# Random-feature attention and a feed-forward block on one core: new start times for the queries, two of four normalisations on ScalarE, and output products two slices behind

## The chip, the core and the metric

The kernel runs on one core of one Trainium2 chip. A core has TensorE (PE: matmuls, with its weight loads as PEld), VectorE (DVE), ScalarE (ACT), GpSimd (POOL) and SyncE (SP), which issues nearly all DMAs here. Each engine works through its own queue in a fixed order, and semaphores hold an instruction until what it reads is there. The metric is the device time of one execution in microseconds (us), lower is better.

## The reference, cut to what matters

```
phi(x): h = x @ omega.T - sum(x*x)/2;  exp(h - max(h)) / sqrt(m)
kv  = einsum('bhsm,bhsd->bhmd', phi(k), v);   z = sum over s of phi(k)
out = einsum('bhsm,bhmd->bhsd', phi(q), kv) / (einsum('bhsm,bhm->bhs', phi(q), z) + 1e-6)
x   = out, heads joined: 4608 x 512
h   = x @ w_in;   g = h - tanh(h);   result = g @ w_out        (w_in 512 x 2048, w_out 2048 x 512)
```

There are 8 batches of 576 tokens and 8 heads of 64; m is 128.

## The kernel before

**Number format.** A float32 value is kept as two parts, a rounded high part and the low rest (`xh`, `xl`; `gh`, `gl`), and a product is three matmuls: high by high, high by low, low by high.

**Attention units.** The work of attention is cut in Python generators that other code advances a step at a time. `k_unit(b, c)` makes, for batch b and head pair c, the matrix `kvw` and the sums `zb`. `q_unit(ch, c)` takes 256 tokens (chunk ch) of a head pair: it loads, splits the input in halves (L132, L133 for the low parts), projects (`pj`), makes the exponentials (L149 on DVE, L153 on ACT), multiplies with `zb` and adds up (L350), takes the reciprocal (L353), scales four 128x128 blocks by it (L359 on DVE, L357 on ACT; the list `norm` says which), transposes on PE (`pt`, L366), splits again (`qh`, `ql`, L385), multiplies with `kvw` (`pn`, L391 and L392) and writes the result to `later` (ACT L396, L397, then DVE L398, L399). `pt` and `pn` share PSUM places, so the next unit's transposes wait until L399 has read this unit's `pn`. `x_split` (L407 on ACT, L408 on DVE) turns a head pair of `later` into `xh` and `xl`, which the feed-forward part reads. `xh` and `xl` hold two chunks: a chunk's number modulo 2 is its place.

**Feed-forward.** Chunks 0 and 1 go together, then chunks 2 to 5 one by one, eight slices each (`ffn_h(ch, s)`: 24 matmuls of 128x256 into a PSUM tile h, L471, then tanh on ACT L475, the subtraction on DVE L476, the two parts by L477 and L478; `ffn_out`: 12 matmuls of 128x512, L489 to L491). Then six pairs of chunks of 512 tokens, the wide part, 16 slices each (`wide_h(a, f)`: 12 matmuls of 128x512, L532, tanh L535, subtraction L536, parts L537, L538, and on POOL L540, L541; `wide_out`: 6 matmuls, L545 to L547; after the 16 slices the other half of the tokens, `last`). The h tiles have two PSUM banks in turn, so a slice's matmuls wait for the subtraction two slices earlier.

**What sets the order.** A counter `t` goes up at each `beat()`, two beats a slice; chunk 2 begins at 32, each chunk takes 16, the wide part begins at 96 and a pair takes 40. `start` holds, for each value of t, the units that begin there. A unit takes a step at every tick after that. `next_x(a)` forces ticks until the eight query units of a pair have ended, and splits them. From these calls a scheduler makes the order of each engine when the program is built; the order is fixed in the program.

Of the kernel before, what the change touches and what calls it, by code (L numbers as in the profile page):

```python
# [19 lines left out]
P = 128  # L20
# [5 lines left out]
C0 = 6  # L26
# [8 lines left out]
def favor_attention_ffn(ctx: ExitStack, tc: tile.TileContext, qT, kT, va, vt, omT, w, out):  # L35
# [283 lines left out]
    def q_unit(ch, c):  # L319
# [68 lines left out]
        for h in range(2):  # L388
            for b, s, e in pieces:
                w = kvs[b, c][0][:, h * P : (h + 1) * P]  # L390
                nc.tensor.matmul(pn[:, h, s:e], w, qh[:, h, s:e], start=True, stop=False)  # L391
                nc.tensor.matmul(pn[:, h, s:e], w, ql[:, h, s:e], start=False, stop=True)  # L392
        while ch >= C0 and gathered < (ch - C0) // 2:
            yield
        xs = later[:, c, ch % 2 * TC : ch % 2 * TC + TC]
        nc.scalar.copy(xs[0:D], pn[D:P, 0])  # L396
        nc.scalar.copy(xs[D:P], pn[0:D, 1])  # L397
        nc.vector.tensor_add(xs[0:D], pn[0:D, 0], xs[0:D])  # L398
        nc.vector.tensor_add(xs[D:P], pn[D:P, 1], xs[D:P])  # L399
        if ch < C0:  # L400
            yield
            x_split(ch, c, xs, nc.vector)
        xdone[ch] = xdone.get(ch, 0) + 1

    def x_split(ch, c, x, engine):
# [121 lines left out]
    def wide_h(a, f):  # L527
        p = ps.tile([P, 2, TC], F32, tag=bank("h"), name=f"h_w{a}_{f}")
        prods = [(w_in(a, f, i, c), x[:, 0:2, c]) for c in range(NC)
                 for i, x in ((0, xh), (0, xl), (1, xh))]  # L530
        for i, (w_, x) in enumerate(prods):
            nc.tensor.matmul(p, w_, x, start=i == 0, stop=i == len(prods) - 1)  # L532
        g = sb.tile([P, 2, TC], F32, tag=bank("o"), name=f"g_w{a}_{f}", bufs=1 if mode["o"][-1] == "g" else 2)
        e = sb.tile([P, 2, TC], F32R, tag="gh", name=f"ge_w{a}_{f}", bufs=2)
        nc.scalar.activation(g, p, AF.Tanh)  # L535
        nc.vector.tensor_sub(g, p, g)  # L536
        nc.scalar.copy(e[:, 0], g[:, 0])  # L537
        nc.vector.tensor_sub(e[:, 1], g[:, 0], e[:, 0].bitcast(F32))  # L538
# [17 lines left out]

    need = {b: (b * S) // TC for b in range(B)}
    xdone = {}
    gathered = 0
    gens = []  # L560

    def tick(new=(), force=False):
# [39 lines left out]
    while decoded < NF:  # L602
# [24 lines left out]
    kvf.clear()  # L627
    ak = open_pool("ak")
    mode.update(
        chain=False, native=False, norm=[nc.vector, nc.vector, nc.vector, nc.scalar], junk=[junk],  # L630
        hi=nc.scalar, pj=["pj0"], pk=["pk"], pt=["pj0"],
        phi=(ak, 3), qh=(ak, 1), ql=(ak, 1), kf=(ak, 1), kx=(ak, 1), qf=(ak, 1),
        qx=(ak, 1), vr=(ak, 1), khl=(ak, 2), vhl=(ak, 2), zs=(ak, 1), c1=(ak, 1), kvs=(ak, 1))
# [5 lines left out]
    def begins(a):  # L639

        return 16 * C0 + 40 * a

    for ch in range(3, NQ):
        a, j = (ch - C0) // 2, (ch - C0) % 2 * NC
        for c in range(NC):
            if ch < C0 + 2:
                k = [(28,32,36,40),(41,45,49,53),(56,60,63,66),(58,68,72,75),(78,81,83,85)][ch - 3][c]
            else:
                k = begins(a - 1) + -9 + 10 * (j + c) // 2
            start.setdefault(k, []).append(("q", ch, c))  # L650
    for b in range(2, B):
        a = ((b * S) // TC - C0) // 2
        for c in range(NC):
            k = [31,51][b - 2] + [5,5][b - 2] * c if b < 2 + len([31,51]) else begins(a - 1) + -18 + 11 * c
            start.setdefault(k, []).append(("k", b, c))
    t = 32 - 2 * (NF - done)
    assert min(start) >= t and all(k == int(k) for k in start)
# [11 lines left out]
    ffn_store(0)  # L669
    mode.update(pj=["pj0", "pj1"], pt=["pt"])  # L670
    prev = None
    for ch in range(2, C0):
        out_tiles(ch)
        for s in range(NS):
            while ch > 2 and xdone.get(ch, 0) < NC:
                tick((), True)
            g = (ch, s, *ffn_h(ch, s))
            beat()
            if prev is not None:
                ffn_out(*prev)  # L680
# [84 lines left out]
```

## Time and profile before

| | us |
|---|---|
| median of three runs | 1074.54 |
| lowest and highest | 1073.91, 1076.31 |
| the profiled execution's own time | 1075.36 |
| its span, first to last instruction | 1073.6 |
| PE busy | 1041.5 |
| DVE busy | 854.3 |
| ACT busy | 695.0 |
| POOL busy | 440.9 |

The profile comes from one execution. Its span and its time differ by 1.8 us. Busy time is the union of an engine's instructions; a matmul's row lasts until its result is written, so two matmuls in a row overlap, and a busy PE has not shown that it lost nothing.

### The profile page before, as it was taken

How to read it: one execution, taken by the hardware profiler on the slowest of the kernel's cores; microseconds unless marked ns; L12 is line 12 of the kernel's file. 1: busy time of each engine (PE TensorE's matmuls, PEld its weight loads, DVE VectorE, ACT ScalarE, POOL GpSimd, SP SyncE). 2: the span in 40 equal slices, each digit the busy share in tenths (PEclk: the TensorE clock that was granted, in tenths of full speed). 3: DMA queues.
4: the chain of work that ended last, by engine and by line, in shares of the span. 5: the costliest groups of instructions: out<-in, count | busy, mean ns of one | idle time of the engine just before them, and what ended most of it. 6: DMA issues, size and time to landing. Idle time of an engine off the chain costs nothing.

```text
span 1073.6 us, 19114 instructions
## 1 busy us (share of the span) xinstructions
PE 1041.5 (97%) x5608; PEld 889.1 (83%) x5608; DVE 854.3 (80%) x3006; ACT 695.0 (65%) x1809; POOL 440.9 (41%) x745
## 2 busy tenths in 40 slices
PE   8988999999999899899999999999999999999998
PEld 7766888999988898688888888888887888888886
DVE  5999995999999989989989888899889958742220
ACT  5997655777777778677767676677666746532220
POOL 3634540544543322556545563656355402221320
PEclk8999999999999999899999999999999999999999
DMA  8952722111211101222234332443243314332301
GB/s 261 295 172 90 283 96 70 33 34 53 55 53 33 53 16 57 72 77 78 78 109 137 103 118 88 130 138 117 65 142 115 104 45 146 114 101 82 104 1 39
DMA packets 85960, 106.18 MB, mean 99 GB/s; under 512 B 17632, under 2 KB 67936, under 8 KB 83808
## 3 DMA queue, kind: packets, MB, share of 16 engines
q1 hardware_dynamic: 85776, 104.92, 31.1%
q8 instruction: 45, 0.74, 0.3%
q14 instruction: 59, 0.48, 0.1%
q10 hardware_dynamic: 80, 0.03, 0.0%
HBM read 87.10 MB, written 17.83 MB: 98 GB/s over the span
## 4 chain that ended last, share of the span: by engine, by line
PE 67%; DVE 22%; issue 5%; ACT 4%; POOL 1%; DMA 0%; DVEq 0%; POOLq 0%; ACTq 0%
PE h_w L532 19%; PE h L471 7%; PE last L545 4%; PE last L547 4%; PE last L546 4%; DVE junk L350 3%; PE po_w L547 3%; PE po_w L546 3%; PE po_w L545 3%; PE po L489 2%; PE po L490 2%; PE po L491 2%; PE pk L269 2%; PE pt L366 2%; DVE phi_q L359 2%
## 5 line engine op out<-in xcount | busy, mean ns | idle before, releaser
L532 PE MATMUL h_w<-xh,w 128*128 128x512 f32 x768 | 253.9, 394 | 2.7 <-DVE g_w L536 2.6
L532 PEld LDWEIGHTS h_w<-xh,w 128*128 128x128 f32 x768 | 144.1, 189 | 31.1 <-DVE g_w L536 4.2
L532 PE MATMUL h_w<-xl,w 128*128 128x512 f32 x384 | 151.3, 394 | 0.9 <-DVE xl L408 0.9
L471 PE MATMUL h<-xh,w 128*128 128x256 f32 (+1 forms) x640 | 147.2, 307 | 3.8 <-DVE g L476 2.2
L540 POOL CAST w<-g_w 128x256 fp32r<-128x256 f32 x96 | 41.0, 427 | 224.2 <-DVE g_w L536 208.5
L471 PEld LDWEIGHTS h<-xh,w 128*128 128x128 f32 x640 | 107.5, 190 | 11.8 <-DVE g L476 3.1
L350 DVE CUSTOM_DVE_ANT_0 junk<-phi_q,zb 128x128 f32<-128x128 f32 (+1 forms) x320 | 105.3, 331 | 13.1 <-ACT phi_q L153 1.0
L536 DVE TENSOR_TENSOR g_w<-h_w,g_w 128x512 f32<-128x512 f32 x96 | 66.0, 687 | 60.6 <-ACT g_w L535 59.9
L471 PE MATMUL h<-xl,w 128*128 128x256 f32 (+1 forms) x320 | 97.5, 305 | 2.1 <-DVE xl L408 2.1
L153 ACT ACTIVATE phi_q<-phi_q,nb_q 128x128 f32<-128x128 f32 x240 | 82.5, 394 | 19.6 <-DVE nb_q L149 18.7
L535 ACT ACTIVATE g_w<-h_w 128x512 f32<-128x512 f32 x96 | 56.8, 591 | 57.1 <-PE h_w L532 53.4
L253 POOL TENSOR_TENSOR khl<-phi_ka,khl 128x256 fp32r<-128x256 f32 x48 | 38.3, 798 | 127.3 <-DVE khl L252 105.5
L532 PEld LDWEIGHTS h_w<-xl,w 128*128 128x128 f32 x384 | 72.8, 190 | 14.4 <-DVE xl L408 1.3
L541 POOL TENSOR_TENSOR w<-g_w,w 128x256 fp32r<-128x256 f32 x96 | 80.0, 833 | 4.6
L440 POOL TENSOR_SCALAR a<-a 128x1024 f32<-128x1024 f32 x14 | 59.0, 4213 | 54.4 <-ACT a L436 36.0
L545 PE MATMUL po_w<-w,ge_w 128*128 128x512 f32 x192 | 75.9, 395 | 0.0
L545 PE MATMUL last<-w 128*128 128x512 f32 x192 | 75.4, 393 | 0.0
L546 PE MATMUL po_w<-w,ge_w 128*128 128x512 f32 x192 | 75.3, 392 | 0.0
L547 PE MATMUL last<-w 128*128 128x512 f32 x192 | 75.2, 392 | 0.0
L546 PE MATMUL last<-w 128*128 128x512 f32 x192 | 75.1, 391 | 0.0
L537 ACT CAST ge_w<-g_w 128x256 fp32r<-128x256 f32 x96 | 39.1, 407 | 55.6 <-DVE g_w L536 53.9
L547 PE MATMUL po_w<-w,ge_w 128*128 128x512 f32 x192 | 72.2, 395 | 1.3 <-DVE ge_w L538 1.2
(173 smaller groups left out, 2911.9 us busy)
## 6 DMA issues: line engine op xcount, KB each, us to landing
w<-w_in SPq DMA_DIRECT2D x320, 128.0 KB, 2.4
raw<-w SPq DMA_DIRECT2D x16, 1024.0 KB, 8.1
kf<-kT SPq DMA_DIRECT2D x32, 288.0 KB, 3.2
qf<-qT SPq DMA_DIRECT2D x72, 128.0 KB, 2.2
out<-o SPq DMA_DIRECT2D x36, 256.0 KB, 2.1
w_in<-w SPq DMA_DIRECT2D x16, 512.0 KB, 3.4
v<-vt SPq DMA_DIRECT2D x24, 288.0 KB, 2.9
v<-va SPq DMA_DIRECT2D x8, 288.0 KB, 5.9
```

The costliest lines, as they stand in the source:

```text
L153: nc.scalar.activation(ph[:, j], ph[:, j], AF.Exp, bias=nb[:, j : j + 1], scale=-1.0)
L350: nc.vector.tensor_tensor_reduce(bank("junk")[r], ph[r, i], kvs[b, c][1][r, h], scale=1.0, scalar=EPS, op0=ALU.mult, op1=ALU.add, accum_ou ...
L440: engine.tensor_scalar(a.bitcast(F32), a.bitcast(F32), 2.0**-15, 122879.9921875, op0=ALU.max, op1=ALU.min)
L471: nc.tensor.matmul(o, w_, x, start=i == 0, stop=i == len(prods) - 1)
L532: nc.tensor.matmul(p, w_, x, start=i == 0, stop=i == len(prods) - 1)
L535: nc.scalar.activation(g, p, AF.Tanh)
L536: nc.vector.tensor_sub(g, p, g)
L540: nc.gpsimd.tensor_copy(hi, g[:, 1])
L541: nc.gpsimd.tensor_sub(lo, g[:, 1], hi.bitcast(F32))
L545: nc.tensor.matmul(o, h, wt[f][:, 0, DM:], start=f == 0, stop=False)
L546: nc.tensor.matmul(o, h, wt[f][:, 1, DM:], start=False, stop=False)
L547: nc.tensor.matmul(o, l, wt[f][:, 0, DM:], start=False, stop=f == NF - 1)
```

## The change

It has five parts. The first two are in the tables of starts: query units of chunks 3 to 9 and key units of batches 2 to 4 begin at other beats. For chunks 3 to 7 (row by row, four head pairs each) and for the key units:

```diff
-k = [(28,32,36,40),(41,45,49,53),(56,60,63,66),(58,68,72,75),(78,81,83,85)][ch - 3][c]
+k = [(28,31,34,37),(43,46,49,52),(40,55,58,63),(61,66,69,72),(75,78,80,83)][ch - 3][c]
...
-                k = begins(a - 1) + -9 + 10 * (j + c) // 2
+                k = begins(a - 1) + (-4 + 9 * (j + c) // 2 if a == 1 else -9 + 5 * (j + c))
...
-            k = [31,51][b - 2] + [5,5][b - 2] * c if b < 2 + len([31,51]) else begins(a - 1) + -18 + 11 * c
+            k = [28,48,82][b - 2] + [5,5,9][b - 2] * c if b < 2 + len([28,48,82]) else begins(a - 1) + -18 + 11 * c
```

The split of a chunk leaves the query unit and is made by the main loop, a slice after the chunk is there; a query unit now writes `later` as soon as the chunk two earlier has been split:

```diff
-        while ch >= C0 and gathered < (ch - C0) // 2:
+        while ch > 3 and ch - 2 not in split:
             yield
...
-        if ch < C0:
-            yield
-            x_split(ch, c, xs, nc.vector)
...
+    def x_of(ch):
+        split.add(ch)
+        for c in range(NC):
+            x_split(ch, c, later[:, c, ch % 2 * TC : ch % 2 * TC + TC], nc.vector)
...
+            if s > 0 and ch + 1 not in split and xdone.get(ch + 1) == NC:
+                x_of(ch + 1)
             g = (ch, s, *ffn_h(ch, s))
+            if ch == C0 - 1 and s == NS - 1 and xdone.get(C0 + 1) == NC:
+                x_of(C0 + 1)
```

Two of a query unit's four normalisations go to ScalarE where one did; the wide part's output products come a slice later, with three places for `e` where there were two and two for `g` where there were three:

```diff
-        chain=False, native=False, norm=[nc.vector, nc.vector, nc.vector, nc.scalar], junk=[junk],
+        chain=False, native=False, norm=[nc.vector, nc.scalar], junk=[junk],
...
-        g = sb.tile([P, 2, TC], F32, tag=bank("o"), name=f"g_w{a}_{f}", bufs=1 if mode["o"][-1] == "g" else 2)
-        e = sb.tile([P, 2, TC], F32R, tag="gh", name=f"ge_w{a}_{f}", bufs=2)
+        g = sb.tile([P, 2, TC], F32, tag="gl", name=f"g_w{a}_{f}", bufs=2)
+        tag = ("gh", "gh", "g")[f % 3]
+        e = sb.tile([P, 2, TC], F32R, tag=tag, name=f"ge_w{a}_{f}", bufs=len(tag))
...
         for f in range(NF):
-            g = wide_h(a, f)
+            behind.append(wide_h(a, f))
             beat()
-            if prev is not None:
-                wide_out(*prev)
+            if f > 1:
+                wide_out(*behind.pop(0))
```

What the scheduler makes of it shows at two places. The first is DVE ahead of the first slice of chunk 4. `later<-pn_4_3` is the last query unit of that chunk, and the `xl_101` behind it its split, for which that slice's last matmuls wait. Before:

```order
L398 TENSOR_TENSOR later_102<-pn_4_3_3512,later_102 64x256
L399 TENSOR_TENSOR later_102<-pn_4_3_3512,later_102 64x256
L252 CAST khl_3_1_0_3525<-phi_ka3_1_3470 128x2x128
L408 TENSOR_TENSOR xl_101<-later_102,xh_100 128x256
L252 CAST khl_3_1_2_3531<-phi_ka3_1_3470 128x2x128
L311 TENSOR_TENSOR kvs_3_0_3581<-pk_3_0_3121,kvs_3_0_3581 128x128
```

and in the changed program, where L405 is what was L408:

```order
L398 TENSOR_TENSOR later_102<-pn_4_3_3583,later_102 64x256
L399 TENSOR_TENSOR later_102<-pn_4_3_3583,later_102 64x256
...
L262 TENSOR_TENSOR vhl_3_1_4_3597<-v_3_1_3257,vhl_3_1_4_3597 64x64
L132 TENSOR_TENSOR qx_5_2_3644<-qf_5_2_3606,qx_5_2_3644 64x256
L262 TENSOR_TENSOR vhl_3_1_4_3597<-v_3_1_3257,vhl_3_1_4_3597 64x64
L133 TENSOR_TENSOR qx_5_2_3644<-qf_5_2_3606,qx_5_2_3644 64x256
...
L262 TENSOR_TENSOR vhl_3_1_5_3700<-v_3_1_3257,vhl_3_1_5_3700 128x2x64
L405 TENSOR_TENSOR xl_101<-later_102,xh_100 128x256
```

One instruction stood between the unit's end and its split; now there are thirteen, of other units, four of them exponent preparations (L149, left out above with their short read-outs).

The second place is PE in the second wide pair. `h_w1_4` is slice 4, `ge_w1_2` what slice 2 hands to its output products. Before:

```order
L532 MATMUL h_w1_4_7421<-xh_100,w8_1133 128x512
L532 MATMUL h_w1_4_7421<-xl_101,w8_1133 128x512
L545 MATMUL po0_w_7140<-w2_448,ge_w1_2_7304 128x512
L305 MATMUL pk_5_1_6948<-ident_64,c1_5_1_7191 128x128 x2
L307 MATMUL pk_5_1_6948<-zhl_5_1_7188,ones_92 128x256 x2
L546 MATMUL po0_w_7140<-w2_448,ge_w1_2_7304 128x512
L547 MATMUL po0_w_7140<-w2_448,ge_w1_2_7304 128x512
```

and in the changed program (L529 was L532, L543 and L544 were L545 and L546):

```order
L529 MATMUL h_w1_4_7423<-xl_101,w9_1243 128x512
L391 MATMUL pn_10_1_7246<-qh_10_1_7207,kvw_4_1_5753 128x256
L392 MATMUL pn_10_1_7246<-ql_10_1_7208,kvw_4_1_5753 128x256
L391 MATMUL pn_10_1_7246<-qh_10_1_7207,kvw_4_1_5753 128x256
L392 MATMUL pn_10_1_7246<-ql_10_1_7208,kvw_4_1_5753 128x256
L145 MATMUL pj_ka5_2_2_7372<-om_89,kx_5_2_7327 128x256 x2
L529 MATMUL h_w1_4_7423<-xh_100,w9_1243 128x512
L543 MATMUL po0_w_7148<-w2_448,ge_w1_2_7306 128x512
L544 MATMUL po0_w_7148<-w2_448,ge_w1_2_7306 128x512
```

The products of slice 2 stood behind the second of slice 4's twelve matmuls; now they stand behind the last one, ten matmuls later.

## Rows read from the trace of the kernel before

**Rows 1.** The page's busy times: us, share of the span, instructions.

```profile
PE 1041.5 (97%) x5608; PEld 889.1 (83%) x5608; DVE 854.3 (80%) x3006; ACT 695.0 (65%) x1809; POOL 440.9 (41%) x745
PE 67%; DVE 22%; issue 5%; ACT 4%; POOL 1%; DMA 0%; DVEq 0%; POOLq 0%; ACTq 0%
```

**Rows 2.** Busy time by stage, stages bounded by ends of L476 or L536.

```profile
core 0: us, PE busy (x) PEld busy (x) DVE busy (x) ACT busy (x) POOL busy (x), PEclk, DMA share, GB/s
215.60:288.90 73.30, 73.07 (x500) 66.80 (x499) 68.83 (x267) 55.30 (x150) 36.23 (x69) 1.00 0.14 42
288.90:382.20 93.30, 88.81 (x601) 80.85 (x600) 85.31 (x354) 70.56 (x194) 35.39 (x67) 1.00 0.17 49
382.20:419.00 36.80, 36.66 (x250) 33.64 (x249) 33.08 (x137) 27.32 (x73) 10.67 (x20) 1.00 0.11 31
419.00:450.20 31.20, 24.99 (x110) 19.17 (x109) 28.99 (x108) 23.19 (x61) 10.74 (x21) 0.89 0.24 74
450.20:553.50 103.30, 103.30 (x542) 87.75 (x541) 92.51 (x361) 72.95 (x203) 54.35 (x104) 1.00 0.25 74
553.50:890.60 337.10, 334.31 (x1732) 281.01 (x1731) 289.96 (x1103) 226.88 (x620) 162.27 (x301) 1.00 0.37 112
```

**Rows 3.** PE's waits over these stages: us in total, times, longest.

```profile
PE h_w L532 <- DVE g_w L536: 2.6, 2, 1.9
PE h L471 <- DVE xl L408: 2.1, 1, 2.1
PE pt L366 <- DVE later L399: 1.7, 2, 1.1
PE po_w L547 <- DVE ge_w L538: 1.2, 2, 0.7
```

**Rows 4.** PE's timeline near 818: start, us.

```profile
818.22 0.40 PE L546 MATMUL po_w<-w,ge_w 128*128 128x512 f32 x1
818.45 0.39 PE L547 MATMUL po_w<-w,ge_w 128*128 128x512 f32 x1
...
819.03 0.28 PE L392 MATMUL pn<-ql,kvw 128*128 128x256 f32 x1
819.15 0.28 PE L391 MATMUL pn<-qh,kvw 128*128 128x256 f32 x1
```

**Rows 5.** Groups over the whole span: busy us, mean ns, idle before.

```profile
L350 DVE CUSTOM_DVE_ANT_0 junk<-phi_q,zb 128x128 f32<-128x128 f32 x256 | 83.9, 329 | 11.5 <-ACT phi_q L153 1.0
L359 DVE TENSOR_SCALAR phi_q<-phi_q,dn 128x128 f32<-128x128 f32 x204 | 58.4, 341 | 1.0
L149 DVE CUSTOM_DVE_ANT_0 phi_q<-pj_q,phi_q 128x128 f32<-128x128 f32 x240 | 57.8, 284 | 4.3 <-ACT phi_q L146 3.5
L262 DVE TENSOR_TENSOR vhl<-v,vhl 128x128 fp32r<-128x128 f32 x96 | 35.6, 371 | 2.0 <-POOL vhl L261 1.2
L357 ACT ACTIVATE phi_q<-phi_q,dn 128x128 f32<-128x128 f32 x84 | 33.2, 420 | 39.9 <-DVE dn L353 39.7
L132 DVE TENSOR_TENSOR qx<-qf,qx 64x256 fp32r<-64x256 f32 x60 | 28.5, 474 | 1.9
L132 DVE TENSOR_TENSOR kx<-kf,kx 64x576 fp32r<-64x576 f32 x24 | 18.6, 774 | 0.8
L408 DVE TENSOR_TENSOR xl<-later,xh 128x256 fp32r<-128x256 f32 x16 | 6.9, 432 | 1.9 <-ACT xh L407 1.7
L535 ACT ACTIVATE g_w<-h_w 128x512 f32<-128x512 f32 x96 | 56.8, 591 | 57.1 <-PE h_w L532 53.4
L536 DVE TENSOR_TENSOR g_w<-h_w,g_w 128x512 f32<-128x512 f32 x96 | 66.0, 687 | 60.6 <-ACT g_w L535 59.9
```

**Rows 6.** Timeline near 380: end of slice 2 of chunk 5, and its subtraction.

```profile
378.46 0.36 PE L471 MATMUL h<-xh,w 128*128 128x256 f32 x1
...
381.48 0.69 DVE L476 TENSOR_TENSOR g<-h,g 128x512 f32<-128x512 f32 x1
```

**Rows 7.** Timelines of DVE and PE near 836.

```profile
836.23 0.43 DVE L538 TENSOR_TENSOR ge_w<-g_w,ge_w 128x256 fp32r<-128x256 f32 x1
...
836.72 0.50 PE L547 MATMUL po_w<-w,ge_w 128*128 128x512 f32 x1 [0.67 <-DVE ge_w L538]
```

More of the change, by code (lines that the diff above doesn't have):

```diff
@@ L558, in favor_attention_ffn @@
     xdone = {}
-    gathered = 0
+    split = {2}
     gens = []
@@ L671, in favor_attention_ffn @@
     prev = None
+    def x_of(ch):
+        split.add(ch)
+        for c in range(NC):
+            x_split(ch, c, later[:, c, ch % 2 * TC : ch % 2 * TC + TC], nc.vector)
     for ch in range(2, C0):
         out_tiles(ch)
+        while xdone[ch] < NC:
+            tick((), True)
+        if ch not in split:
+            x_of(ch)
         for s in range(NS):
-            while ch > 2 and xdone.get(ch, 0) < NC:
-                tick((), True)
+            if s > 0 and ch + 1 not in split and xdone.get(ch + 1) == NC:
+                x_of(ch + 1)
             g = (ch, s, *ffn_h(ch, s))
+            if ch == C0 - 1 and s == NS - 1 and xdone.get(C0 + 1) == NC:
+                x_of(C0 + 1)
             beat()
@@ L689, in favor_attention_ffn @@
     ffn_store(C0 - 1)
-    mode.update(o=["g", "gl"])
+    mode.update(o=["gl"])
     def next_x(a):
-        nonlocal gathered
-        for ch in (C0 + 2 * a, C0 + 2 * a + 1):
+        pair = (C0 + 2 * a, C0 + 2 * a + 1)
+        for ch in pair:
             while xdone.get(ch, 0) < NC:
                 tick((), True)
-        gathered = a + 1
-        for c in range(NC):
-            x_split(slice(0, 2), c, later[:, c].rearrange("p (j t) -> p j t", j=2), nc.vector)
+        if split.isdisjoint(pair):
+            for c in range(NC):
+                x_split(slice(0, 2), c, later[:, c].rearrange("p (j t) -> p j t", j=2), nc.vector)
+            split.update(pair)
+        for ch in pair:
+            if ch not in split:
+                x_of(ch)
     next_x(0)
@@ L704, in favor_attention_ffn @@
         out_tiles("w")
-        prev = None
+        behind = []
         for f in range(NF):
-            g = wide_h(a, f)
+            behind.append(wide_h(a, f))
             beat()
-            if prev is not None:
-                wide_out(*prev)
+            if f > 1:
+                wide_out(*behind.pop(0))
             i = NF * a + f + 6
@@ L714, in favor_attention_ffn @@
             beat()
-            prev = g
-        wide_out(*prev)
+        for g in behind:
+            wide_out(*g)
         for i in range(2):
```

## The prediction, before the changed kernel ran

> **What bounds the kernel now.** I read the busy times first. PE is busy for 97% of the span and the chain that ended last lies on PE for 67% and on DVE for 22% [rows 1]: a TensorE kernel with stretches where DVE decides. Next come the windows, cut where DVE ends the subtraction of a slice: chunk 2 slice 5, chunk 3 slice 6, chunk 5 slices 2 and 7, wide slice 2 of the first pair, wide slice 0 of the second, wide slice 0 of the fifth [rows 2]. I call them stages 1 to 6. In stages 1 to 4 DVE is busy 94, 91, 90 and 93% of the time. Stages 5 and 6 have DVE at 90 and 86% and PE at or near 100%. Then PE's waits: the four longest groups all name DVE, by a subtraction, a split, a query result and an output part [rows 3].
>
> A busy PE hides losses, so I count its work instead. A 128x512 matmul starts 0.23 us after the one ahead of it and a 128x256 one 0.12 us [rows 4]. The order has, for stage 4, 60 wide ones, 45 of 256 and 14 transposes: 13.8 + 5.4 + 1.4 = 20.6 us of work in 31.2 us. That is the worst place, 10.6 us lost. It is the start of the wide part, where the eight query units of chunks 6 and 7 must have ended. The clock is 0.89 there, between the levels 2.4 and 1.2 GHz: at the low one for 22% of 31.2, or 6.9 us. Stage 5 has 360, 136 and 40: 102 to 103 us in 103.3, nothing lost. Stage 6 has 1152, 368 and 214 narrow ones: about 326 us, times 1.01 for what stage 5 shows as usual, 329 to 330 in 337.1: 7 us lost.
>
> **The change, part by part.** The start tables move work between stages, and only the built order tells how much. I count DVE's instructions between the same subtractions in both orders, and price them by busy time over count [rows 5]: L149 0.24 us, L350 0.33, L359 0.29, L262 0.37, half a query's split (L132 or L133) 0.475, half a key's 0.775, L408 0.43, and 0.43 for each of the rest (casts, L385, L398 and the like). The moved L359s are in these counts.
>
> Stage 1: 4 fewer L149, 5 fewer L359, 2 fewer key halves, 3 fewer L262, two fewer others: -1.0 - 1.45 - 1.55 - 1.1 - 0.85 = -5.9 us. Stage 2: 10 more L149, 4 more L350, 4 query halves, 2 key halves, 3 L262, 3 L408 and 3 others, 5 fewer L359: 2.4 + 1.3 + 1.9 + 1.55 + 1.1 + 1.3 + 1.3 - 1.45 = +9.4. Stage 3: 12 fewer L149, 4 L359, 4 query halves, 2 key halves, 3 L262 and one L350, five fewer others, one split more: -2.9 - 1.15 - 1.9 - 1.55 - 1.1 - 0.3 - 2.15 + 0.45 = -10.6. Stage 4: 7 fewer L359, 5 L350, 4 query halves, 3 splits (three double ones become three single), against 2 more L149, 2 key halves, 2 L262 and one other: -2.0 - 1.65 - 1.9 - 1.3 + 0.5 + 1.55 + 0.75 + 0.4 = -3.65. In all -10.7 us ahead of the wide part's steady run, 6.1 of it the 21 L359s.
>
> Elapsed times from these [rows 2]. Stage 1: (68.8 - 5.9) / 0.94 = 67.0, and PE's work there, 66.0 times 1.01, is no longer than that: **-6.3**. Stage 2: DVE has 94.7 us against 90 on PE, so DVE decides. At stage 4's busy share, 93%, it takes 101.9: **+8.6**. The bounds are 0, if DVE's 8.0 idle us there take up what is added, and +10.3 at today's share. I take the higher half because the first place of the orders shows why DVE can't use its idle time: it waits at chunk starts for a chain of units. Stage 3: DVE is left with 22.5 us and PE with 33.4, so PE decides. It comes in ahead of DVE by 3.4 us (a slice's matmuls end at 378.82, its subtraction at 382.17) [rows 6] and leaves ahead by a tanh and a subtraction, 0.59 + 0.69 = 1.3 [rows 5]: 33.8 - 3.4 + 1.3 = 31.7, **-5.1**. Bounds: 24 if DVE could decide, 33.8. Stage 4: (29.0 - 3.65) / 0.93 = 27.3, **-3.9**; bounds 0, if the chain of the last two query units sets it, and -7.3, if the clock holds as well. Stage 5: 12 more 256 matmuls, **+1.0**.
>
> Stage 6 keeps its matmuls. What it loses comes from a DVE that lags: output products wait 0.67 us for a part that ends at 836.66 [rows 7], h tiles wait for a subtraction [rows 3]. The third edit puts the products ten matmuls later, 2.3 us of cover. The moved normalisation takes DVE work away there too: 8 units a pair, one L359 of 0.29 each. The h tiles get no cover from the later products, only from a DVE that lags less. I take **-5.0** of the 7 lost; bounds -2 (the waits of rows 3 alone) and -7.
>
> Costs at nothing: eight single splits for four double ones, counted above. ScalarE takes 60 more L357 of 0.42 us, 25 us on an engine idle 35% of the span [rows 1, 5]; its wait for the reciprocal, 39.7 us in all, is there already, and a second operation behind it waits no more. If that cover fails it is a rival, below. Two places for g instead of three: POOL and ScalarE read g for under 2 us of a slice of about 5.4, so I price it at 0; the bound is one POOL delay in each pair, under 0.5 us each.
>
> At ScalarE the Trainium skill speaks against the change. "ScalarE: Activation LUTs", section Rules for kernel authors, says that multiplies belong on VectorE rather than ScalarE. The rows agree on the single operation: 0.42 us there and 0.34 here from start to end [rows 5]. By the page the move would cost 0.08 times 60, about 5 us of engine time. What counts is which of the two engines is full, and that is DVE in stages 1 to 4.
>
> The sum: -6.3 + 8.6 - 5.1 - 3.9 + 1.0 - 5.0 = -10.7. The profiled execution took 1075.36, so 1064.7; the median is 0.8 lower, so 1063.9, rounded **1064**. Ahead of stage 1 the orders are the same up to chunk 2's first slice, and the last 75 matmuls are the same: 0 for both ends.
>
> **The rivals.**
>
> *Stage 2 swallows its load.* DVE's 8.0 idle us there take all of the 9.4, and with less waiting PE keeps the full clock at the wide part's start. Then 8.6 and up to 3.4 (half of 6.9) fall away: 1052 to 1056. For it: DVE idles 8% there. Against it: the waits are chains. Of the clock the profile shows 0.89 in the one stage where PE idles for 20% of the time [rows 2]. "TensorE: Matmul & The Clock Gate", section What's actually happening, says that being throttled is the default and that activity lifts it; so fewer gaps there could give the 3.4 back. Chance 0.18.
>
> *The later products are there already.* The second place of the orders shows that the scheduler had put them behind slice f+2's first two matmuls, and the h tiles still wait. Then stage 6 gives 1 and stage 4's chain 0: 1063.9 + 4 + 3.9 = 1072. Chance 0.11.
>
> *Slower: the last query unit of chunks 4 and 5 comes late.* Thirteen instructions now stand between that unit and its split at chunk 4, where one stood. If both chunk starts lose what the wide part's start loses today, 10.6 each, against about 5 that stage 2 loses now, 16 more are lost instead of 8.6, and stage 4, which has the same chain, keeps its 3.9: 1063.9 + 7.4 + 3.9 = 1075; and if the clock falls at both, 3.4 each, 1082. It turns slower when stage 2 takes 19 us more than before. Chance 0.08.
>
> *Slower: ScalarE becomes what is waited for.* By the same mechanism as the page's rule: 21 operations of 0.42 stand in front of tanhs in stages 1 to 4, 8.8 us on the path, and the 6.1 taken from DVE do not show: 1079. Against it: ACT is busy 75% there, 55.3 of 73.3 in stage 1. Chance 0.03.
>
> *Nothing moves on balance:* the chunks give back what the wide part gains, 1074. Chance 0.05.
>
> **How the numbers follow.** The forecast, 1060 to 1069, has 0.55. The range 1054 to 1072 holds it, most of the first rival (0.15) and of the second (0.10): 0.80. A measurement of this kernel can tell 0.2%, about 2.1 us, from no change. Faster than 1072.4: 0.55 + 0.18 + 0.11 = 0.84. Same: 0.05. Slower than 1076.7: 0.08 + 0.03 = 0.11.
>
> **What the changed profile would show.** Between the same subtractions the stages take about 67, 102, 32, 27, 104 and 332 us; stage 2 is the test of the whole, since it alone should be longer. PE waits for a split at the start of chunk 4. L357 runs 144 times at about 0.42 and L359 144 times. In stage 6 PE's waits for L538 are gone and those for L536 are shorter. The prediction is wrong if DVE turns out not to be the pace of stages 1 to 4, so that counting its work says nothing, or if ScalarE appears among PE's waits.

## The result, and the profile after

| | us |
|---|---|
| the changed kernel, median of five runs | 1078.58 (1077.93 to 1081.46) |
| the kernel before, on the same chip, five runs | 1074.89 (1073.91 to 1076.31) |
| ratio of the two | 1.0041, 95% interval 1.0028 to 1.0053 |
| predicted | 1064, range 1054 to 1072 |

The change is slower by 0.4%; its profiled execution took 1078.58, with a span of 1076.8. The page after, busy times and the shares of the chain that ended last:

```profile
PE 1042.3 (97%) x5608; PEld 888.0 (82%) x5608; DVE 845.8 (79%) x2950; ACT 712.3 (66%) x1873; POOL 444.0 (41%) x745
PE 66%; DVE 22%; ACT 7%; issue 3%; POOL 2%; DMA 0%; DVEq 0%; ACTq 0%; POOLq 0%
```

DVE has lost 8.5 us of work and ScalarE has got 17.3 [rows 1]. The windows of the six stages, cut where DVE ends the same subtractions as in [rows 2]:

```profile
core 0: us, PE busy (x) PEld busy (x) DVE busy (x) ACT busy (x) POOL busy (x), PEclk, DMA share, GB/s
216.30:285.60 69.30, 67.44 (x463) 61.85 (x461) 63.30 (x248) 54.56 (x149) 31.23 (x59) 1.00 0.15 44
285.60:388.10 102.50, 98.29 (x652) 88.98 (x651) 96.13 (x392) 80.17 (x223) 38.07 (x72) 0.98 0.15 46
388.10:418.20 30.10, 30.10 (x205) 27.75 (x204) 24.82 (x94) 20.77 (x54) 5.39 (x11) 1.00 0.05 14
418.20:449.30 31.10, 27.74 (x137) 21.97 (x136) 25.57 (x94) 23.54 (x64) 15.47 (x27) 0.95 0.28 85
449.30:557.40 108.10, 105.33 (x536) 86.34 (x535) 94.87 (x365) 77.53 (x218) 56.77 (x106) 1.00 0.24 74
557.40:893.30 335.90, 334.18 (x1740) 282.52 (x1739) 287.99 (x1096) 235.17 (x650) 164.63 (x302) 1.00 0.37 112
```

| stage | before | predicted | after | difference: predicted, measured | measured by PE's own ends |
|---|---|---|---|---|---|
| 1 | 73.3 | 67.0 | 69.3 | -6.3, -4.0 | +0.2 (69.1 to 69.3) |
| 2 | 93.3 | 101.9 | 102.5 | +8.6, +9.2 | +4.8 (95.5 to 100.3) |
| 3 | 36.8 | 31.7 | 30.1 | -5.1, -6.7 | -2.4 (36.3 to 33.9) |
| 4 | 31.2 | 27.3 | 31.1 | -3.9, -0.1 | -5.2 (32.7 to 27.5) |
| 5 | 103.3 | 104.3 | 108.1 | +1.0, +4.8 | +7.4 (103.2 to 110.6) |
| 6 | 337.1 | 332 | 335.9 | -5.0, -1.2 | -2.2 (337.4 to 335.2) |

The last column cuts the same stages where the last matmul of the bounding slice ends on PE. The two cuts differ by how far DVE's subtraction lags behind PE there, 1.4 to 5.6 us before, and that lag changed too: in stage 1 it is longer at the start (3.2 us, 1.4 before) and shorter at the end (3.2, 5.6 before), and PE gained nothing.

Cut at the subtractions, stages 1 to 3 sum to -1.5 where -2.8 was predicted, and most of the 14 us that are missing lies in stages 4 to 6: -7.9 predicted, +3.5 measured. By PE's own ends stage 5 is the largest single miss, +7.4 where +1.0 was predicted. PE's longest waits over the six stages, and one further down that list:

```profile
PE pj_km L145 <- ACT kvs L310: 2.0, 1, 2.0
PE h L468 <- DVE g L473: 2.0, 4, 0.8
PE pj_kb L145 <- DVE vhl L262: 1.7, 1, 1.7
PE pk L269 <- POOL khl L253: 1.1, 3, 0.7
PE pt L366 <- DVE later L399: 1.1, 3, 0.5
PE pj_kb L145 <- DVE nb_km L149: 0.8, 1, 0.8
PE po_w L545 <- DVE ge_w L536: 0.7, 1, 0.7
```

Before, three of the four longest were feed-forward matmuls that waited for feed-forward results or splits [rows 3]. Now most are attention units' own matmuls (`pj`, `pk`, `pt`) that stand at the head of PE's queue before their input, or their place in PSUM, is there. (L545 and L536 are what were L547 and L538.)

A view that does not move with DVE's lag is the **time that PE loses**: for each matmul its distance in the trace to the one ahead, less the usual distance of that pair of kinds (the lower third over the traces compared), summed up between PE's own ends of the slices that bound the stages. It holds waits, the overlap that is missing behind each (rows of about 0.4 us that otherwise start 0.23 apart [rows 4]), and stretches at the lower clock. It goes by profiled executions, one each:

| kernel | time, us | ratio to before, interval | 1 | 2 | 3 | 4 | 5 | 6 | after 6 | sum |
|---|---|---|---|---|---|---|---|---|---|---|
| before | 1074.9 | | 2.7 | 9.0 | 1.2 | 12.5 | 1.8 | 12.3 | 1.0 | 40.5 |
| changed | 1078.6 | 1.0041 (1.0028 to 1.0053) | 3.8 | 11.2 | 0.7 | 7.7 | 7.8 | 10.3 | 2.3 | 43.8 |
| e1 normalisation alone | 1079.5 | 1.0048 (1.0035 to 1.0061) | 1.0 | 10.7 | 0.8 | 12.3 | 6.0 | 13.4 | 1.0 | 45.2 |
| e2 later products alone | 1072.4 | 0.9984 (0.9975 to 0.9993) | 2.8 | 11.7 | 0.9 | 11.7 | 2.2 | 9.5 | 1.0 | 39.8 |
| e3 starts and split alone | 1077.3 | 1.0036 (1.0024 to 1.0048) | 4.5 | 14.1 | 1.2 | 6.7 | 3.8 | 11.6 | 1.0 | 42.9 |
| e4 all but later products | 1077.6 | 1.0030 (1.0019 to 1.0040) | 3.8 | 11.7 | 0.7 | 8.3 | 6.7 | 10.9 | 1.0 | 43.1 |
| e5 another one on ScalarE | 1073.4 | 0.9987 (0.9978 to 0.9997) | 2.4 | 7.4 | 0.9 | 10.0 | 2.3 | 16.0 | 0.9 | 39.9 |
| e6 another two on ScalarE | 1074.3 | 0.9996 (0.9987 to 1.0005) | 1.1 | 7.7 | 0.9 | 12.1 | 4.0 | 12.3 | 1.0 | 39.1 |
| e7 changed, old wide starts | 1087.3 | 1.0110 (1.0096 to 1.0125) | 3.8 | 12.9 | 0.7 | 11.4 | 6.9 | 13.5 | 2.3 | 51.5 |
| e8 changed, chunk 4 earlier | 1080.6 | 1.0051 (1.0038 to 1.0064) | 6.6 | 8.9 | 0.8 | 12.6 | 4.6 | 9.6 | 2.3 | 45.4 |
| e9 changed, another two | 1078.7 | 1.0038 (1.0025 to 1.0050) | 3.8 | 12.2 | 1.1 | 9.2 | 1.3 | 17.0 | 0.9 | 45.5 |
| e12 none on ScalarE | 1081.3 | 1.0064 (1.0050 to 1.0078) | 4.0 | 12.0 | 0.8 | 10.3 | 5.7 | 13.7 | 0.9 | 47.4 |
| e13 e1's work, order held | 1073.8 | 0.9996 (0.9987 to 1.0004) | 2.9 | 8.5 | 1.0 | 12.4 | 2.2 | 12.3 | 1.0 | 40.3 |
| e15 e2's work, order held | 1077.8 | 1.0033 (1.0022 to 1.0044) | 2.8 | 10.5 | 0.9 | 10.3 | 3.6 | 15.0 | 1.0 | 44.1 |
| e18 e2's order, e1's work | 1070.8 | 0.9965 (0.9951 to 0.9978) | 2.8 | 8.5 | 0.9 | 10.1 | 2.6 | 8.8 | 1.0 | 34.7 |

The kernels from e1 on are told below; they ran on three chips, and each ratio is to the kernel before on the same chip. For the change: stage 4 does lose 4.8 us less, as forecast, and stage 6 loses 2.0 less; stage 5 loses 6.0 more, stage 2 loses 2.2 more, stage 1 1.1 and the end 1.3.

### The profile page after: what moved, and what is told of

The parts are those of the page before. It is cut to its first block, busy times and chain, and to the rows that moved or that the text cites. A ratio compares the mean times of both kernels' runs of the same rounds, so it can differ in the third digit from the quotient of the medians.

```text
span 1076.8 us, 19123 instructions
## 1 busy us (share of the span) xinstructions
PE 1042.3 (97%) x5608; PEld 888.0 (82%) x5608; DVE 845.8 (79%) x2950; ACT 712.3 (66%) x1873; POOL 444.0 (41%) x745
## 3 DMA queue, kind: packets, MB, share of 16 engines
q1 hardware_dynamic: 85776, 104.92, 31.1%
## 4 chain that ended last, share of the span: by engine, by line
PE 66%; DVE 22%; ACT 7%; issue 3%; POOL 2%; DMA 0%; DVEq 0%; ACTq 0%; POOLq 0%
PE h_w L529 19%; PE h L468 7%; PE last L545 4%; PE last L544 4%; PE last L543 4%; DVE junk L350 3%; PE po_w L545 3%; PE po_w L543 3%; PE po_w L544 3%; PE po L486 2%; PE po L487 2%; PE po L488 2%; PE pj_q L145 2%; PE pk L269 2%; PE pt L366 2%
## 5 line engine op out<-in xcount | busy, mean ns | idle before, releaser
L529 PE MATMUL h_w<-xh,w 128*128 128x512 f32 x768 | 259.1, 393 | 1.1 <-DVE g_w L534 1.1
L529 PEld LDWEIGHTS h_w<-xh,w 128*128 128x128 f32 x768 | 143.0, 189 | 27.5 <-DVE g_w L534 1.7
L529 PE MATMUL h_w<-xl,w 128*128 128x512 f32 x384 | 150.6, 392 | 0.0
L538 POOL CAST w<-g_w 128x256 fp32r<-128x256 f32 x96 | 41.3, 430 | 219.1 <-DVE g_w L534 169.3
L350 DVE CUSTOM_DVE_ANT_0 junk<-phi_q,zb 128x128 f32<-128x128 f32 (+1 forms) x320 | 109.4, 343 | 13.3 <-ACT phi_q L153 1.3
L468 PEld LDWEIGHTS h<-xh,w 128*128 128x128 f32 x640 | 108.1, 191 | 14.1 <-DVE g L473 5.1
L533 ACT ACTIVATE g_w<-h_w 128x512 f32<-128x512 f32 x96 | 56.7, 592 | 49.7 <-PE h_w L529 49.2
L529 PEld LDWEIGHTS h_w<-xl,w 128*128 128x128 f32 x384 | 72.4, 189 | 13.7 <-DVE xl L405 0.8
L535 ACT CAST ge_w<-g_w 128x256 fp32r<-128x256 f32 x96 | 39.1, 407 | 57.7 <-DVE g_w L534 57.0
L543 PE MATMUL po_w<-w,ge_w 128*128 128x512 f32 x192 | 75.3, 392 | 0.2 <-ACT ge_w L535 0.2
L545 PE MATMUL last<-w 128*128 128x512 f32 x192 | 75.4, 393 | 0.0
L543 PE MATMUL last<-w 128*128 128x512 f32 x192 | 75.2, 392 | 0.0
L544 PE MATMUL last<-w 128*128 128x512 f32 x192 | 75.1, 391 | 0.0
L357 ACT ACTIVATE phi_q<-phi_q,dn 128x128 f32<-128x128 f32 x144 | 50.8, 407 | 36.6 <-DVE dn L353 35.9
L544 PE MATMUL po_w<-w,ge_w 128*128 128x512 f32 x192 | 75.0, 391 | 0.0
L545 PE MATMUL po_w<-w,ge_w 128*128 128x512 f32 x192 | 74.2, 391 | 0.7 <-DVE ge_w L536 0.7
```

What stands on the lines that cost most here:

```text
L350: nc.vector.tensor_tensor_reduce(bank("junk")[r], ph[r, i], kvs[b, c][1][r, h], scale=1.0, scalar=EPS, op0=ALU.mult, op1=ALU.add, accum_ou ...
L357: e.mul(ph[:, i], ph[:, i], dn[:, i : i + 1])
L468: nc.tensor.matmul(o, w_, x, start=i == 0, stop=i == len(prods) - 1)
L543: nc.tensor.matmul(o, h, wt[f][:, 0, DM:], start=f == 0, stop=False)
L544: nc.tensor.matmul(o, h, wt[f][:, 1, DM:], start=False, stop=False)
L545: nc.tensor.matmul(o, l, wt[f][:, 0, DM:], start=False, stop=f == NF - 1)
```

## The experiments

**One part at a time.**

```diff
 e1, on before
-norm=[nc.vector, nc.vector, nc.vector, nc.scalar], junk=[junk],
+norm=[nc.vector, nc.scalar], junk=[junk],
 e2, on before: the two hunks of the change in wide_h and in the loop over f
 e3, on before: the start tables, split, x_of and next_x of the change
 e4, on the changed kernel: the hunks of e2 taken back
```

> The kernel before, with only the normalisation changed to two of four blocks on ScalarE. Three theories of why the whole change came out at 1078.6 where 1064 was forecast. A, the starts: the new start times put so much into chunk 3 and so much into the second pair of chunks that what the other parts gain is used up; then this kernel gains what the forecast gave to the moved multiplications, 4 to 6 us, 1069 to 1071. B, the later output products: they let DVE run 5 to 6 us behind PE instead of 1 to 5, and attention's own chains then hold up PE; then this kernel gains the same, 1069 to 1071. C, the multiplication on ScalarE makes the chain of a query unit longer and PE waits for it: 1076 to 1080. A and B agree here and are told apart by the other two.

> The kernel before, with only the wide part's output products one slice later (and the places for g and e that go with it). Up to the start of the wide part at 450 us it should be as before within 1 us. A: a gain in stage 6 of 2 to 5 us, 1070 to 1073. B: 1077 to 1082, with DVE's subtractions in the wide part ending 5 to 6 us behind the matmuls of their slice, and new waits of PE for results of attention units there. If the scheduler had put the products that late already: 1074 to 1076.

> The kernel before, with only the new start tables and the split of a chunk made by the main loop; normalisation and output products as before. A: 1078 to 1086, since it has the longer stage 2 without the gain of the other two parts. B: 1066 to 1072. C: 1066 to 1072 as well.

> The changed kernel, with the output products of the wide part one slice behind again and everything else kept. A: 1079 to 1083, a loss against the changed kernel's 1078.6 since the later products gain. B: 1065 to 1071. C: 1077 to 1080, no difference to the changed kernel that can be told.

Measured: 1079.5, 1072.4, 1077.3, 1077.6. The part that was to gain on ScalarE costs 5.0 us by itself; A and B both fall with it. (e2 came out as A had it, e1 and e4 as C had it; e3 missed all three ranges.) The later products gain 2.1, the starts lose 2.8. The sum, +5.7 by the medians and +7.3 by the ratios, is more than the whole, +3.7 and +4.4, though by little more than the intervals allow.

**Amount or order?** Another choice of the blocks that ScalarE scales leaves the amounts alone and makes the scheduler rebuild the order.

```diff
 e5, on before: one of four, but the first
+norm=[nc.scalar, nc.vector, nc.vector, nc.vector], junk=[junk],
 e6, on before; e9, on the changed kernel: two of four, but the last two
+norm=[nc.vector, nc.vector, nc.scalar, nc.scalar], junk=[junk],
 e12, on before: none
+norm=[nc.vector], junk=[junk],
```

> The kernel before; the one normalisation of four that ScalarE does is the first of a unit instead of the last. No engine has more or less to do. The norm-only kernel was 5 us slower than before. Theory C, a count: two operations on ScalarE where one was make the chains longer; then this kernel stays within 1.5 us of before, 1073 to 1076. Theory D, an order: any edit makes the scheduler weave the attention units into the matmuls in another way, and the way of before was a good one, so that most changes lose some us at the starts of chunks and pairs; then this kernel moves by 2 to 5 us though it does the same work, most likely to 1076 to 1080.

> The kernel before with two of four normalisations on ScalarE, as in the changed kernel, but the last two of a unit instead of the second and the fourth. Engine times are those of the norm-only kernel that took 1079.5. C: 1078 to 1081 again. D: another weaving, so another time, anywhere from 1070 to 1080 and more than 2 us away from 1079.5, with the lost PE time at other slices.

> The changed kernel, with the last two normalisations of a unit on ScalarE instead of the second and the fourth. Amounts on every engine are those of the changed kernel. Theory Q: amounts decide, and the new starts and later products are what costs: 1077 to 1080, no difference to the changed kernel. Theory O: the order that the scheduler weaves decides; on the kernel before the same swap was worth 5 us (1079.5 against 1074.3). If the second and fourth are worse in themselves, the gain comes here too: 1072 to 1075. If each order is an accident of its own: anywhere from 1070 to 1083, more than 2 us away from 1078.6.

> The kernel before with all four normalisations on DVE: 60 more operations of 0.29 us there, 21 of them in stages 1 to 4, 60 fewer on ScalarE. Q, the way in which the forecast priced the change (DVE's work in stages 1 to 4 over its busy share): 6.1 us more DVE work there and some in the first pairs, so 1080 to 1083, the mirror of the 6.1 us that the change takes away. O: the 6 us need not show; 1071 to 1079.

Measured: 1073.4, 1074.3, 1078.7, 1081.3. e5 stayed where C had it and not where D did, but e6 rules C out: it has the amounts of e1 and is 5.2 us faster. In e1's order 2639 of PE's 5432 matmul instructions stand at another place than before, by up to 35 places. e9 has the time of the changed kernel, but loses 1.3 us in stage 5 where that lost 7.8, and 17.0 in stage 6 where it lost 10.3: the loss moved. e12 agrees with the forecast's arithmetic (1080 to 1083), which proves little, since a rebuilt order alone is worth as much.

**The starts.**

```diff
 e7, on the changed kernel
-k = begins(a - 1) + (-4 + 9 * (j + c) // 2 if a == 1 else -9 + 5 * (j + c))
+k = begins(a - 1) + -9 + 10 * (j + c) // 2
 and the third entry of the key table (82, 9) taken out
 e8, on the changed kernel
-(28,31,34,37),(43,46,49,52),(40,55,58,63)
+(28,31,34,37),(41,44,47,50),(40,55,58,63)
```

> The changed kernel, with the starts in the first wide pair as before: key units of batch 4 and query units of chunks 8 and 9. In the changed kernel PE loses 6.2 us between slices 3 and 15 of the first wide pair, where it lost 1.0 before. If the later, denser starts there are the cause: that loss falls to 1 to 2 us and the time to 1073 to 1075. If the moved normalisation or the order as such is the cause: the loss stays at 4 to 6 us there, and the time at 1077 to 1080.

> The changed kernel, with the four query units of chunk 4 two beats earlier (41, 44, 47, 50 instead of 43, 46, 49, 52). In the changed kernel PE loses 6.0 us in the first slice of chunk 4, where it waits for the split of that chunk's last unit and drops to the lower clock; before it lost 0.3 there. If the last unit is late because it starts late: the loss falls to under 2 us and the time to 1073 to 1075. If DVE simply has too much to do in stage 2, whatever the order: the loss moves to the next slices, stage 2 stays at 101 to 103 us and the time at 1077 to 1080.

Measured: 1087.3 and 1080.6, both slower than the changed kernel and outside every range given. Taking the later wide starts back doesn't help: the time rises by another 8.7 us. In e8 the loss of the first slice of chunk 4 falls from 6.0 to 2.3 us, but slices around it lose more than they did, and the wide part's start loses 12.6 instead of 7.7. The loss at chunk 4 depends on the starts; curing it there moves it elsewhere.

**The same work, the order held.** These kernels tie every instruction to the one that stood ahead of it on its engine, by a dependency without a wait, in the order of the kernel named; only the edited instructions move. (Their line numbers are higher, since the orders stand in the file as lists.)

```diff
+for places in ORDERS:                       # one list for each engine
+    for i, j in zip(places, places[1:]):
+        tc.add_manual_dep(traced[j], traced[i].name, NoSync)
```

e13 holds before's order with e1's work, e14 with e6's, e15 with e2's (products of slice f where those of f+1 stood, and e2's places for `g` and `e`), e17 with e1's and e2's. e16 holds the changed kernel's order and takes the normalisation back to DVE. e18 holds the order that the scheduler made for e2 and adds e1's work.

> The kernel before with the second and fourth normalisation of a unit on ScalarE, as in the norm-only kernel that was 5 us slower, but with the order of every engine held as it was before: dependencies without a wait tie each instruction to the one that stood ahead of it, and the moved multiplication stands on ScalarE right ahead of the one that was there already. Theory O, the new order lost the time and the moved work is a gain in itself, as the forecast had it: 1068 to 1072. Theory C, the multiplication costs more on ScalarE than it frees on DVE: 1077 to 1080. Theory N, the moved work is worth nothing either way, and only the order decides: 1074 to 1076.

> The same with the last two normalisations of a unit on ScalarE. With the order left to the scheduler the two choices were 5.2 us apart. O and N: with the order held they are within 1 us of each other. If the choice of the two multiplications matters by itself: some 5 us faster than the other held kernel.

> The kernel before with the later output products, with the order of every engine held but for those products: slice f's six matmuls stand where slice f+1's stood. Left to the scheduler the edit was worth 2.1 us. O as the forecast had it: stage 6 gains 5 us of the 7 that it loses, 1069 to 1071. If the products were late enough already: 1074 to 1076.

> The changed kernel with three of four normalisations on DVE again, in the order of the changed kernel: the multiplication that goes back stands on DVE right behind the unit's first. O: DVE has 6.1 us more to do in stages 1 to 4 and 0.29 us for each unit later, so 1082 to 1086. C: a gain, 1073 to 1076. N: 1077 to 1080.

Measured: e13 1073.8 (0.9996); e14 1074.0, ratio 0.9998 (0.9990 to 1.0007); e15 1077.8 (1.0033); e16 1082.3, ratio 1.0072 (1.0059 to 1.0084). e13 is N's case (0.2 us below its range), e14 came out as expected, e15 is slower than either range, and e16 is O's. In the traces of e13 and e14 the rows of PE, its weight loads, DVE, ACT and POOL stand in before's order, the multiplications apart. The two choices of blocks that were 5.2 us apart are now the same: what e1 lost, 0.52% or 5.6 us against e13, came from its order. (No kernel tied before's order and moved nothing, so a cost of the ties alone is not measured; the traces have the same number of these rows, and PE loses 40.3 us in e13 and 40.5 before.) The moved work itself is worth 0.04% in before's order, and 0.31% or 3.3 us in the changed kernel's (1.0072 less 1.0041, give or take 0.18%). e13's windows, the same stages:

```profile
214.00:287.30 73.30, 72.93 (x497) 66.59 (x497) 67.95 (x262) 56.69 (x155) 35.92 (x68) 1.00 0.15 42
287.30:380.10 92.80, 88.96 (x602) 80.97 (x601) 84.69 (x346) 72.38 (x201) 36.25 (x68) 1.00 0.17 49
380.10:416.50 36.40, 36.40 (x249) 33.54 (x248) 32.45 (x133) 28.34 (x78) 10.91 (x20) 1.00 0.11 32
416.50:447.40 30.90, 24.38 (x109) 18.83 (x108) 28.20 (x105) 23.91 (x64) 10.96 (x21) 0.89 0.23 72
447.40:551.60 104.20, 104.20 (x545) 88.30 (x544) 91.11 (x353) 75.37 (x211) 55.10 (x104) 1.00 0.24 75
```

DVE's counts in the first four are 5, 8, 4 and 3 below [rows 2]: 20 multiplications left these stages, 5.8 us at the forecast's 0.29. DVE's busy time fell by 2.9 us only, 0.15 each. The rows of neighbours overlap, and the last of a run costs what it adds; the same unit before and in e13:

```profile
311.39 0.67 DVE L359 TENSOR_SCALAR phi_q<-phi_q,dn 128x128 f32<-128x128 f32 x3
310.28 0.48 DVE L668 TENSOR_SCALAR phi_q<-phi_q,dn 128x128 f32<-128x128 f32 x2
```

The third adds 0.2 us to two; busy time over count is not the price of one. The stages' times went from 73.3, 93.3, 36.8 and 31.2 to 73.3, 92.8, 36.4 and 30.9, by 1.2 us together, and stage 5 took 0.9 longer. By PE's own ends the six stages take 674.0 us in e13 and 674.3 before, though DVE is busy 10.1 us less over the whole run (844.2 and 854.3). In this order, being busy 90 to 94% of a stage does not make DVE what sets its length.

e15's waits of PE from slice 2 of the first wide pair to the end of stage 6:

```profile
PE h_w L839 <- DVE g_w L844: 1.3, 3, 0.7
PE pj_ka L452 <- DVE nb_q L456: 0.9, 2, 0.6
PE pj_kb L452 <- DVE nb_km L456: 0.7, 1, 0.7
PE pj_kb L452 <- DVE nb_ka L456: 0.4, 1, 0.4
PE pt L673 <- ACT phi_q L453: 0.3, 1, 0.3
PE pj_q L452 <- DVE nb_kb L456: 0.3, 1, 0.3
```

The waits of output products for their parts, 1.2 us [rows 3], are gone, as forecast. But h tiles and attention's own matmuls wait 3.9 us in these rows, where all of PE's waits in the same stretch before sum to 2.5. Most are `pj` matmuls that need one of the projections' two PSUM places, which DVE's exponent preparation (`nb`) has to read first. A likely reason, argued and not shown by itself: the products that moved back were work that PE did while DVE got there. With six fewer matmuls ahead of them, 1.4 us by the distance of [rows 4], attention's matmuls come to the head of the queue earlier. The edit's other half, fewer places for `g`, shows in no row of the waits as a wait for a place.

> The kernel before with both edits of work, normalisation and later output products, in the held order of before (products of slice f where those of slice f+1 stood). Held, the one was worth -0.5 us and the other +3.5. If edits add up as long as the order isn't rebuilt: 1076.5 to 1078.5. If the normalisation gains more once the products are late, as the forecast had it (DVE lags less, and the products no longer wait): 1071 to 1075.

> The fastest kernel so far, before with the later output products and the order that the scheduler made for them (1072.4), with that order held and the second and fourth normalisation moved to ScalarE. If the moved work is worth what it was worth in the order of before, 0.5 us: 1071 to 1073, faster than both kernels. If it is worth what it is in the order of the changed kernel, 3.7 us: 1068 to 1070.

Measured: e17 1076.5, ratio 1.0018 (1.0009 to 1.0027), against 1.0029 for the sum of e13 and e15: additive to within the intervals, at the edge of what was expected. With the order rebuilt nothing of the sort holds. Two more kernels joined e2's later products with a choice of blocks that by itself had gained or done nothing:

> The kernel before with the later output products (alone 2.1 us faster) and the last two normalisations on ScalarE (alone within 1 us of before). If gains add up: 1071 to 1073, the fastest yet with the later products alone. O: they don't add; 1069 to 1079, and the parts that gained alone need not gain here.

> The kernel before with the later output products and the one ScalarE normalisation as the first of a unit (alone 1.4 us faster). If gains add up: 1070 to 1072. O: 1069 to 1079.

e10 took 1076.5, ratio 1.0014 (1.0005 to 1.0022); e11 1077.3, ratio 1.0022 (1.0013 to 1.0031). e11's two parts had gained 2.1 and 1.4 us and lose 2.4 together. e18, in an order that was kept, took 1070.8, 0.9965: 4 us faster than before and 8 faster than the change. That is 0.19% below e2 (give or take 0.16%), between its two expected ranges: the moved work is worth about 2 us in this order. Two of its stages:

```profile
417.30:447.50 30.20, 24.54 (x116) 19.39 (x115) 28.17 (x105) 23.41 (x63) 10.98 (x21) 0.94 0.26 78
550.10:884.20 334.10, 333.62 (x1738) 282.44 (x1738) 284.36 (x1092) 234.59 (x650) 166.53 (x303) 1.00 0.37 112
```

Stage 4 runs at a clock of 0.94 instead of 0.89, and stage 6 is 3.0 us shorter than before; e2's own stage 6 took 334.9, so most of that came with its order.

## Why the prediction was wrong, step by step

**The step that failed** is the one from counted work to time. Stages 1 and 4 were priced by "DVE's work over its busy share", stage 6 by a DVE with less to do, and stage 5 by PE's extra matmuls alone, with the loss there left at nothing. The counts themselves were near: DVE was to have 62.9, 94.7, 22.5 and 25.4 us of work in stages 1 to 4 and had 63.3, 96.1, 24.8 and 25.6. Together that is 6.4 us less than before where 10.7 was forecast; one cause is the price of 0.29 us for a moved multiplication, which adds 0.2. The elapsed times did not follow: DVE's share is 0.91 in stage 1 and 0.82 in stage 4, not 0.94 and 0.93. What the runs show in its place is the order: with before's order held the moved work changes PE's six stages by 0.3 us (e13), with the order rebuilt the same work costs 5.6 us (e1).

**Stage 1**, -6.3 predicted, -4.0 measured: all of it is the changed lag of DVE at the two cuts. PE took 69.3 us where it had taken 69.1.

**Stage 2**, +8.6 predicted, +9.2 measured: the size is right, in part by luck, since 4.8 of it is on PE and the rest a change of DVE's lag at the two cuts. PE does lose time at the start of chunk 4, where the forecast saw a wait for a split. The timeline there, DVE and PE:

```profile
305.07 0.43 DVE L399 TENSOR_TENSOR later<-pn,later 64x256 f32<-64x256 f32 x1
...
306.20 0.42 DVE L132 TENSOR_TENSOR qx<-qf,qx 64x256 fp32r<-64x256 f32 x1
...
307.99 0.51 DVE L405 TENSOR_TENSOR xl<-later,xh 128x256 fp32r<-128x256 f32 x1
```

```profile
306.19 0.62 PE L145 MATMUL pj_kb<-om,kx 128*128 128x256 f32 x2 [1.74 <-DVE vhl L262]
306.61 0.80 PE L468 MATMUL h<-xh,w 128*128 128x256 f32 x2
...
308.58 0.56 PE L468 MATMUL h<-xl,w 128*128 128x256 f32 x1
```

```profile
302.00:306.00 4.00, 2.15 (x15) 1.60 (x13) 3.67 (x19) 3.38 (x11) 3.42 (x10) 1.00 0.00 0
306.00:310.00 4.00, 3.63 (x15) 3.23 (x16) 3.81 (x20) 3.91 (x11) 0.37 (x2) 0.57 0.10 33
```

The last query unit ends at 305.50, the low part of its split at 308.50, and PE's first matmul on it starts at 308.58: the thirteen instructions in between, most of them of other units, took their 2.5 us. But the long wait of PE, 1.74 us, is not for the split. It ends at 306.19, with a key unit's L262, which stood behind the query unit's L399 and two exponent preparations in DVE's queue. PE, idle for nearly half of the four microseconds from 302, gets the clock at 0.57 for the next four, close to its lower level of 1.2 GHz, and does its matmuls slowly until the split is there. The rival of the late unit had the place and the lower clock; it happened at chunk 4, where PE lost 6.0 us instead of 0.3, and not at chunk 5 (1.5 instead of 3.5). Its threshold, 19 us more in stage 2, was not reached.

**Stage 3**, -5.1 predicted, -6.7 measured: PE decides, as argued: the forecast gave it 33.8 us, and by its own ends it took 33.9. The lag at the two cuts makes the rest.

**Stage 4**, -3.9 predicted, -0.1 measured. PE did lose 4.8 us less, 7.7 against 12.5, but that did not reach the end of the stage: slice 2's matmuls ended at 444.2, and their subtraction 5.1 us later where it was 2.3 before. ScalarE's queue shows why:

```profile
447.39 0.70 ACT L153 ACTIVATE phi_q<-phi_q,nb_q 128x128 f32<-128x128 f32 x2 [2.60 <-DVE nb_q L149]
448.00 0.58 ACT L533 ACTIVATE g_w<-h_w 128x512 f32<-128x512 f32 x1
```

The slice's tanh (L533) stood behind a query unit's exponentials, and these waited for a DVE that was at other work in its queue until then. What PE gained it lost again in **stage 5** (+1.0 predicted, +4.8 measured, +7.4 by PE's own ends), which I took for full because I saw no loss there before. PE's waits there after:

```profile
PE pj_kb L145 <- DVE nb_km L149: 0.8, 1, 0.8
PE pj_ka L145 <- ACT qx L78: 0.5, 1, 0.5
PE pj_q L145 <- DVE nb_ka L149: 0.5, 2, 0.3
PE pt L366 <- DVE later L399: 0.5, 1, 0.5
PE po_w L543 <- ACT ge_w L535: 0.2, 1, 0.2
```

They sum to 2.5 of the 7.8 us lost; the rest is the missing overlap behind each and short stretches that no row names. With the order held the normalisation costs stage 5 0.4 us (2.2 lost against 1.8), with it rebuilt 4.2 (6.0).

**Stage 6**, -5.0 predicted, -1.2 measured. The waits for L538 are not gone, as I had said: one of 0.7 us is left (L545 for L536, above), where there were two of 1.2 together [rows 3]. And the later products are no cover by themselves: held, they cost 3.5 us (e15), and only a rebuilt order makes them a gain of 2.1 (e2). I had counted the ten matmuls that they move past as cover for the products, and not asked whose cover they had been.

**Cost at nothing: places and order in the last pair.** In the changed kernel the last pair's slice 2 follows slices 0 and 1 without products between, and waits until its PSUM bank is free:

```profile
990.75 0.50 PE L529 MATMUL h_w<-xh,w 128*128 128x512 f32 x1 [1.07 <-DVE g_w L534]
```

PE loses 1.4 us there, where I had said that the end is the same.

**ScalarE.** The groups of the normalisation after:

```profile
L357 ACT ACTIVATE phi_q<-phi_q,dn 128x128 f32<-128x128 f32 x144 | 50.8, 407 | 36.6 <-DVE dn L353 35.9
L359 DVE TENSOR_SCALAR phi_q<-phi_q,dn 128x128 f32<-128x128 f32 x144 | 43.7, 348 | 1.4
```

144 of each, as predicted, and the wait for the reciprocal did not grow (35.9, 39.7 before). ScalarE does head PE's waits after (2.0 us, `pj_km` for L310), which the forecast had named as a sign of being wrong. But e16, which has the changed order and one normalisation of four on ScalarE again, shows the same wait, so it belongs to the order and not to the moved operations:

```profile
PE pj_km L455 <- ACT kvs L620: 2.0, 1, 2.0
```

The rival that ScalarE becomes what is waited for would have given 1079, close to the measured time, and is refuted all the same: with the order held, 60 more operations on ScalarE cost nothing (e13) and taking them back costs 3.3 us (e16). Nor did they make the unit longer: from the reciprocal to the end of its last multiplication the median of the 60 units fell from 1.31 us before to 1.04 in e13. The Trainium skill, "ScalarE: Activation LUTs", section Rules for kernel authors, prefers VectorE for multiplies. A single one is slower on ScalarE here too, 0.41 us against 0.35, but no two runs here in the same order show a gain from keeping it off; in a held order it is free or a gain.

**What stays open.** Why one rebuilt order is good and another bad was not predicted and can't be read from the trace of the kernel before. The starts can't be run with the order held, since they are an order themselves; so their +2.8 us holds both their own worth and what the scheduler made of the rest. Of the 18.1 us that PE loses in stages 5 and 6 of the changed kernel, the rows of its waits name 3.7.

## What to carry to other kernels

Where a scheduler makes the order, an edit of a few operations rebuilds it, and here that alone cost up to 5.6 us, more than the work that was edited was worth: hold the order and edit the work by itself before believing either sign. A busy share of 90% does not make an engine the pace, and its rows overlap: take a few of its operations away in the held order and see how much busy time goes and whether the stage gets shorter. Cut stages at the engine whose time you want to explain, since a lag at the cut looks like a gain. And work that is moved away from a wait may have been what another wait was hidden behind.

## What was not expected of the hardware

e2 has the orders of PE and DVE of the kernel before, row for row, up to slice 2 of the wide part, yet its profiled stage 2 shows a clock of 0.96 where [rows 2] have 1.00:

```profile
288.10:382.20 94.10, 89.61 (x591) 81.90 (x590) 85.42 (x354) 70.02 (x192) 35.18 (x67) 0.96 0.16 49
```

It is at the lower level from 365.7 on for 6.8 us, at the start of chunk 5, and lost 11.7 us in the stage against 9.0. What PE did ahead of it was nearly the same in both; first e2, then the kernel before:

```profile
362.00:365.70 3.70, 1.81 (x13) 1.34 (x11) 3.57 (x11) 2.29 (x7) 2.18 (x3) 1.00 0.00 0
365.70:372.50 6.80, 6.15 (x29) 6.15 (x30) 6.05 (x26) 4.06 (x11) 2.87 (x5) 0.50 0.37 108
362.70:366.40 3.70, 1.92 (x13) 1.42 (x12) 3.57 (x11) 2.41 (x7) 2.18 (x3) 1.00 0.00 0
366.40:373.20 6.80, 6.02 (x51) 6.02 (x52) 6.30 (x28) 4.61 (x13) 2.89 (x5) 1.00 0.41 108
```

In the same order, and after the same half-idle stretch, the lower clock came in one execution and not in the other. Executions of one and the same program differ too: the fifteen of the kernel before beside e18 have mean clocks of 0.991 to 0.995. So one trace tells a stage's loss to some 3 us only (11.7 and 9.0 here), and the medians decide.
